# Attention and two expert layers in one kernel: ranking steps of the second layer later, its second phase in pieces, and another order of the last attention slots

## The chip, the cores and the metric

The kernel runs on one core of one Trainium2 chip. The metric is the time of one execution on the device, in microseconds (us). All matrix products run on TensorE (PE); VectorE (DVE), ScalarE (ACT) and GpSimd (POOL) do the elementwise work; SyncE (SP) issues most of the DMA transfers, POOL the indirect ones.

## The reference, cut to what matters

Three stages, each on the output of the one before. Attention has 2 batches, 8 heads, 576 positions and 64 features a head, with a causal mask and a decay bias; its output is read as 1152 tokens of 512 features.

```python
# stage 1: attention, per batch and head
scores = where(causal, -1e9, q @ k.T / 8 + minimum(bias(s), 0))
x = softmax(scores) @ v                    # -> x [1152, 512]

# stage 2: one expert a token, at most 288 tokens an expert, in token order
expert_idx = argmax(x @ w_gate, 1);  gate_w = softmax(x @ w_gate)[expert_idx]
y = relu(disp @ w1[e]) @ w2[e]             # E=8, D=512, F=1024
x = gate_w * y, rows scattered back        # 0 for a token that found no place

# stage 3: tokens and experts matched in order of falling logits
order = argsort(-(x @ w_gate2).flatten())
for idx in order:                          # token is free and the expert has under 144
    assign(token, expert)
out[mask] = relu(x[mask] @ w1[e]) @ w2[e]
```

## The kernel before, in words

Every engine runs its own instructions in the order in which the program issues them, and that order is written out by hand. There are three stages.

**Attention** goes in slots, one head each, numbered m = -7 to 18. The lists `ORDER[0]` and `ORDER[1]` (even and odd slots) name the pieces of a slot in their order: E0 to E3 are scores and their exponentials (`pE`, L528 on PE, `pf`, L536 on ACT), M and D the running maxima for a later head (`pM`, D on DVE at L488, which writes `rm`), G0 the scaling of `rm` on ACT (L494), V0 to V2 the product with v (`pog`, L559 to L564), R0 to R2 the normalization (`rs` L570, `rs` L573, `xs` L578 on DVE; R2 frees the `pog` bank for the V0 of the slot after). P0 and P1 make the second half of a split of the exponentials (`ph` L403, `pl` L414; `pl` is on POOL for some). X1 splits a finished head pair into two f16 halves, `XR`, one on ACT (L401), one on POOL (L414).

The gate of batch 0 is a generator, `gate0`, and one of its steps is run behind each piece of slots 11 and 12 (`step0`, GATE0 = 11); `WAITS` says behind which piece a marked step may go on. Its row work is on DVE: `gg` L703 to L709, the counts `cnt` L782, the ranking of experts to L789 (`eri`), then `slot` and the gate's inverse (L720 to L726). `cnt` reads the counts out of the `pog` bank. Then the tokens of batch 0 are scattered to `xd` in DRAM by five indirect DMAs (`scatter`, places in `SCATTER0`) in slots 13 to 15. `zero_fill` sets the DRAM buffers `xd` and `x2d` to zero, two transfers a slot (none in slot 9), on SP; `W0` says how many quarters of the first expert's weights are asked for after which slot, on the same queue, and `SPA` how many weight splits go behind a slot. A split makes `wh` (f16, ACT, L160) and `wl` (bf16, DVE, L164) of an f32 quarter `wf`, so that a product runs as three 16-bit passes (L1004 to L1006).

**First expert layer**: eight experts with 288 places, PE nearly without a break.

**Second expert layer**: eight experts with 144 places, taken in order of how soon they are full. The matching runs as phases p = 0 to 7 of the generator `work`. One phase multiplies indicators by gate rows (L1651 to L1667, into `px`; `g` is made by ACT L1659 and DVE L1661 out of `rowb`, L1224, which ACT copies from PE's transposes L1221), compares (L1869 to L1878), makes places (L1504 to L1512) and counts (L1885 on PE, `tot` L1888), finds which expert is full (`evi` L1679, read by SP to load weights), multiplies again for its tokens (L1518, L1902, `tok` L1715), which POOL gathers into `xg` (L1523), and PE transposes (`spread`, L1543, `xt` L1548).

An expert is 4 groups of 24 products into a hidden layer (L1004 to L1006), then the second layer, L1948, in 4 output blocks. In the first expert a block is 8 f32 products (16 records in the trace); with `halved` = 4 it is 12 f16 and 4 f32 products (20 records). Between these pieces `tick(k)` runs what a script says for place k (0 to 11 in the first product, 12 to 21 in the second): `w` is one step of `work`, `h` and `l` the next ACT and DVE part of a weight split, `s` and `t` the halves of the next expert's `spread`, `0` and `1` the halves of the last expert's output. `FIRST` is the script of the first expert, `THEN` that of all others.

## Time and profile before

| | us |
|---|---|
| three runs: lowest, median, highest | 442.37, 442.89, 448.96 |
| profiled execution, its own time | 441.93 |
| its span on the core | 440.1 |
| PE busy (share of the span) | 396.0 (90%) |
| DVE, ACT, POOL busy | 333.6, 261.8, 191.1 |
| mean granted TensorE clock | 0.973 |

The profile's times start at the span's start. Slot 11 begins at about 96.6 us, slot 12 at 102.1, 13 at 110.7, 14 at 118.0, 15 at 124.2; the first expert layer runs from 147.5 to about 290 us, and the second from 297.7 to 432 us. A matmul's record is longer than its distance to the next, because matmuls overlap: the distance of two starts is the time that one takes.

### The profile page before, as it was taken

To read this page: it belongs to the slowest core of one execution; us is meant where nothing else is said; L and a number is where in the kernel's file an instruction comes from. 1 tells how busy PE (TensorE), PEld (TensorE's weight loads), DVE (VectorE), ACT (ScalarE), POOL (GpSimd) and SP (SyncE) were. 2 spreads that over 40 slices of the span, in tenths; PEclk is the share of its full clock that TensorE was granted. 3 is DMA by queue.
4 is the path that set the end of the run, shared out by engine and by line. 5 is a ranking of instruction groups with operands and counts; after the bars stand their busy time and mean duration, and the time that the engine had idled before them with its cause. 6 is when DMAs were issued, how large, how long until landed. Compare 5 with 4: busy or idle time off the path is not lost.

```text
span 440.1 us, 13965 instructions
## 1 busy us (share of the span) xinstructions
PE 396.0 (90%) x5376; PEld 366.0 (83%) x5376; DVE 333.6 (76%) x955; ACT 261.8 (59%) x472; POOL 191.1 (43%) x306
## 2 busy tenths in 40 slices
PE   1679999998878799999999999869989999999994
PEld 1457888886766799999999999738879999999993
DVE  7889999989677377867778894858596878876730
ACT  4448888876482255556565853535476776766641
POOL 4397788875770702142044181522054244244121
PEclk9979999999899999999999999988989999999998
DMA  6797899952987869999999691188999697899511
GB/s 153 168 216 166 181 212 225 224 148 81 311 290 234 298 158 306 384 343 343 335 346 391 99 174 20 29 251 218 356 359 343 200 354 281 242 334 345 171 41 35
DMA packets 94399, 103.04 MB, mean 234 GB/s; under 512 B 56136, under 2 KB 63304, under 8 KB 94323
## 3 DMA queue, kind: packets, MB, share of 16 engines
q1 hardware_dynamic: 88931, 91.85, 71.6%
q0 software_dynamic: 4192, 9.91, 7.3%
q8 instruction: 44, 0.72, 0.7%
q10 hardware_dynamic: 1200, 0.30, 0.3%
q14 instruction: 32, 0.26, 0.2%
HBM read 81.42 MB, written 14.59 MB: 218 GB/s over the span
## 4 chain that ended last, share of the span: by engine, by line
PE 57%; DMA 14%; DVE 13%; issue 6%; ACT 4%; SPq 3%; POOL 2%; POOLq 0%; DVEq 0%; ACTq 0%
PE C L1061 11%; DMA xg<-x2d,tok 7%; PE A L1004 4%; PE A L1005 4%; PE A L1006 4%; PE pog L559 3%; PE C L1948 3%; PE pT L452 3%; DVE wl L164 3%; PE pM L476 2%; PE pE L528 2%; DMA wf<-in_moe_w_dram 2%; PE pE L529 2%; DVE wf L164 2%; PE A L1948 2%
## 5 line engine op out<-in xcount | busy, mean ns | idle before, releaser
L164 DVE TENSOR_TENSOR wl<-wf,wh 128x1024 bf16<-128x1024 f32 x64 | 77.0, 1222 | 22.7 <-ACT wh L160 22.2
L160 ACT ACTIVATE wh<-wf 128x1024 f16<-128x1024 f32 x64 | 65.7, 1050 | 18.5 <-DMA wf<-in_moe_w_dram 10.5
L1005 PE MATMUL A<-xt,wh 128*128 128x144 f16 (+4 forms) x288 | 59.5, 231 | 0.0
L1006 PE MATMUL A<-xt,wl 128*128 128x144 f16 (+4 forms) x288 | 59.5, 231 | 0.0
L1004 PE MATMUL A<-xt,wh 128*128 128x144 f16 (+4 forms) x288 | 59.5, 231 | 0.0
L1061 PE MATMUL C<-h,wf 128*128 128x160 f32 (+7 forms) x544 | 58.3, 269 | 0.0
L1176 POOL DMA_INDIRECT x2d<-xo,tix x14 | 22.9, 1638 | 71.2 <-DVE l L1193 26.5
L1004 PEld LDWEIGHTS <-wh 128*128 128x128 f16 x512 | 50.6, 99 | 2.2 <-PE pM L653 1.6
L1005 PEld LDWEIGHTS <-wh 128*128 128x128 f16 x512 | 50.4, 99 | 1.5 <-issue 1.0
L1006 PEld LDWEIGHTS <-wl 128*128 128x128 bf16 x512 | 50.5, 99 | 0.0
L536 ACT ACTIVATE pf<-pE,XB 128x512 f32<-128x512 f32 (+4 forms) x80 | 36.9, 514 | 10.5 <-PE pE L531 10.3
L414 POOL TENSOR_TENSOR pl<-pf,ph 128x512 f16<-128x512 f32 x30 | 35.6, 1196 | 11.4 <-DVE ph L403 8.8
L1972 POOL DMA_INDIRECT out_dram<-x2f,tok x14 | 16.2, 1160 | 55.4 <-ACT h L1012 26.3
L164 DVE TENSOR_TENSOR wf<-wf,wf 128x1024 bf16<-128x1024 f32 x30 | 35.7, 1218 | 2.6 <-ACT wf L160 2.6
L1523 POOL DMA_INDIRECT xg<-x2d,tok x16 | 24.9, 1556 | 26.3 <-PE A L1221 11.2
L1061 PEld LDWEIGHTS C<-h,wf 128*128 128x128 f32 x256 | 36.2, 190 | 0.0
L488 DVE CUSTOM_DVE_ANT_0 junk<-pM,cb 128x128 f16<-128x128 f32 (+4 forms) x80 | 32.1, 430 | 4.6 <-PE pM L478 3.9
L476 PE MATMUL pM<-al,ar 128*128 128x128 f16 (+2 forms) x96 | 26.5, 317 | 7.1 <-DVE rm L488 6.9
L1948 PE MATMUL C<-h,wf 128*128 128x144 f32 (+1 forms) x312 | 32.6, 260 | 0.0
L160 ACT ACTIVATE wf<-wf 128x1024 f16<-128x1024 f32 x30 | 31.3, 1051 | 0.0
L559 PE MATMUL pog<-vf,pf 128*128 128x65 f32 x180 | 29.1, 284 | 0.0
L1006 PE MATMUL C<-xt,wl 128*128 128x144 f16 x128 | 25.1, 229 | 0.0
(431 smaller groups left out, 1190.0 us busy)
## 6 DMA issues: line engine op xcount, KB each, us to landing
wf<-in_moe_w_dram SPq DMA_DIRECT2D x128, 512.0 KB
xd<-zero SPq DMA_DIRECT2D x18, 257.0 KB
cb<-cumd SPq DMA_DIRECT2D x16, 288.0 KB
x2d<-zero SPq DMA_DIRECT2D x9, 260.5 KB
kf<-in_k_dram SPq DMA_DIRECT2D x16, 128.0 KB
vf<-in_v_dram SPq DMA_DIRECT2D x16, 128.0 KB
qf<-in_q_dram SPq DMA_DIRECT2D x14, 128.0 KB
bl<-al SPq DMA_DIRECT2D x16, 72.0 KB
```

Of the source, the lines that this page charges most:

```text
L160: nc.scalar.activation(hi, src, AF.Copy)
L164: nc.vector.tensor_sub(lo, src, hi)
L414: (nc.gpsimd if ENG[name][i % 2] == "P" else nc.vector).tensor_sub(o, x, y)
L476: nc.tensor.matmul(o, AR[m][:, t * P:(t + 1) * P], AL[m][:, j0:j1], start=True, stop=not diag)
L488: nc.vector.tensor_tensor_reduce(junk[:w, :j1 - j0], o, CB[m][:w, j0:j1], 1.0, r if t == 4 and j0 == 0 else -3e38, OP.add, OP.max, r)
L536: nc.scalar.activation(d, o, AF.Exp, bias=x, scale=2.0 ** -13)
L559: nc.tensor.matmul(o, pf[:, c:c + P], VF[n % 4][:, j, h], start=False, stop=j == t)
L1004: nc.tensor.matmul(ph[:, g], wh[:, c, fs], xt[:, c], start=c == 0, stop=False)
L1005: nc.tensor.matmul(ph[:, g], wh[:, c, fs], xt[:, 4 + c], start=False, stop=False)
L1006: nc.tensor.matmul(ph[:, g], wl[:, c, fs], xt[:, c], start=False, stop=c == 3)
L1061: nc.tensor.matmul(py[:, g], a[:, f, d], b[:, f], start=k == 0, stop=k == len(terms) - 1)
L1948: nc.tensor.matmul(py[:, g], a[:, f, d], b[:, f], start=k == 0, stop=k == len(terms) - 1)
```

## The change

**Attention.** G0 stands behind D3 in both lists, so `rm` is scaled after the copies `al` and `ar`. The gate of batch 0 makes `slot` and the inverse only when slot 12 has reached its last piece, S, behind the normalization of that slot; the weights are asked for inside the gate, as soon as `eri` is known, four quarters, then 2 and 2 (`W0`); `x2d` is zeroed in slots 9 to 11 with 3 transfers each, not between the weights. The splits behind slots 13 to 15 are 2, 1, 1 (`SPA`), not 1, 1, 2. The next-to-last X1 goes before the fourth of the five scatters, not behind the fifth place.

**Second expert layer.** The w2 of the first expert comes in quarters of rows (2 x 512 values a partition), not of columns (8 x 128). Expert 1 is no longer `halved`: two splits fewer and f32 products in its second layer. Phase 1 is in pieces: its comparisons and counts stand between the halves of expert 0's spread, its places and tokens later. In expert 2 and after, a phase's products stand behind all four groups of the hidden layer (place 10), not behind three (place 8), and counts, tokens and the transposes L1221 are each 2 to 4 places later. A new script `SECOND` is for expert 1.

The diff, cut to its core:

```diff
-        if i // 2 == E:
+        if i == 2 * E:
             sl = (slice(None), slice(None), slice(c * f // 4, (c + 1) * f // 4))
...
-    second_splits = [(2 * E + i, part) for i in range(2 * E) for part in range(HALF2 // 2 if i % 2 else 4) if i != 1]
+    second_splits = [(2 * E + i, part) for i in range(2 * E) for part in range(HALF2 // 2 if i % 2 else 4) if i not in (1, 3)]
...
-    SPA = {13: 1, 14: 1, 15: 2}
+    SPA = {13: 2, 14: 1, 15: 1}
...
         yield from first_experts()
+        some_w(W0[GATE0 + 1])
         yield "loads"
         yield from gate_rows(0)
...
-    WAITS = {"products": (GATE0, "M2"), "sums": (GATE0, "R0"), "loads": (GATE0 + 1, "V2")}
+    WAITS = {"products": (GATE0, "M2"), "sums": (GATE0, "R0"), "loads": (GATE0 + 1, "S")}
-    W0 = {GATE0 + 1: 3, GATE0 + 2: 3, GATE0 + 3: 2}
+    W0 = {GATE0 + 1: 4, GATE0 + 2: 2, GATE0 + 3: 2}
...
-        if m in (GATE0, GATE0 + 1):
+        if GATE0 <= m < GATE0 + 3:
...
-        "E0 Q E1 K X1 M0 D0 V0 M1 V1 D1 X QE M2 VS XE E3 P0 D2 P1 QS E2 V2 R0 R1 G0 M3 T R2 D3 XG VT TE L LG G1 LV S".split(),
-        "E0 VS M0 V0 Q D0 M1 E1 D1 P0 P1 V1 X1 E3 K E2 QE M2 V2 D2 R0 M3 X T R1 G0 LG XE TE R2 D3 QS L S G1 VT XG LV".split(),
+        "E0 Q E1 K X1 M0 D0 V0 M1 V1 D1 X QE M2 VS XE E3 P0 D2 P1 QS E2 V2 R0 R1 M3 T R2 D3 XG VT TE G0 L LG G1 LV S".split(),
+        "E0 VS M0 V0 Q D0 M1 E1 D1 P0 P1 V1 X1 E3 K E2 QE M2 V2 D2 R0 M3 X T R1 LG XE TE R2 D3 G0 QS L S G1 VT XG LV".split(),
...
+                    if (m, name) == (NH - 2, "S"):
+                        x1(NPAIR - 2)
                     scatter(0, slice(n, n + 1))
...
-            x1(NPAIR - 2)
             first_ones()
...
-        if m >= 0 and m != 9:
-            zero_fill(2)
+        if m >= 0:
+            zero_fill(2 if m < 9 else 3)
...
+            if p == 1:
+                yield
+                in_turn(counts, ranked)
+                known(p)
+                yield
+                in_turn(places)
+                kept_ranks()
+            else:
+                in_turn(counts, [None] + left)
+                known(p)
...
-            halved = HALF2 if e else 0
+            halved = HALF2 if e > 1 else 0
...
-    FIRST = "w . lw . . w . w w w w . w . wh l w h st lh wl hll"
-    THEN = "w h l h l0 w w . w . h w1l h wl h . w l s tl h l"
+    FIRST = "w . l . . w w . . . . www w . wh l h w st wlh wl hll"
+    SECOND = ". . . . 0 w w w . . w 1 h wl h . wl h ls tl wh l"
+    THEN = "w h l h l0 w w . . . wh 1l h wl h . w l s tl wh l"
...
-    XT1[0] = spread(xg.pop(0), between=(3, 2))
+    XT1[0] = spread(xg.pop(0), between=(ranked_first, counted_first))
```

On DVE, in slot 12 at the gate of batch 0, one piece of the difference (`L578` is R2 of the head before, `L488` is D3):

```order
 L570 TENSOR_SCALAR rs<-pog 128x5
-L703 TENSOR_TENSOR gt_2168<-pog,OH 128x40
+L703 TENSOR_TENSOR gt_2172<-pog,OH 128x40
 L573 RECIPROCAL rs<-rs 128x5
-L705 TENSOR_REDUCE gg<-gt_2168 128x5
+L705 TENSOR_REDUCE gg<-gt_2172 128x5
+L578 TENSOR_TENSOR xs_168<-pog,rs 128x5x64
 L707 TENSOR_SCALAR gg<-gg 128x5
-L578 TENSOR_TENSOR xs_168<-pog,rs 128x5x64
-L709 SCALAR_TENSOR_TENSOR gg<-gg 128x5
 L488 ISA junk,rm_159<-pM,cb,rm_159 64x512
 L488 ISA rm_159 64x1
```

`xs` stands ahead of L707 now, and L709 behind the maxima, right before `cnt` L782.

On DVE at the start of expert 0 of the second layer, where phase 1 goes from its comparisons to its counts; before:

```order
L1507 TENSOR_SCALAR hq_5795<-r_5790 128x5
L1508 SCALAR_TENSOR_TENSOR hq_5795<-hq_5795,r_5790 128x5
L1509 TENSOR_TENSOR hq_5795<-hq_5795,Lr 128x5
L1510 TENSOR_TENSOR O_5796<-iota0f,hq_5795 128x360
L1512 TENSOR_TENSOR hq_5795<-Lr,hq_5795 128x5
L1504 TENSOR_TENSOR R_5797<-BA_5787,hq_5795 128x40 x2
L164 TENSOR_TENSOR wl_84<-wf_78,wh_83 128x4x256
L1888 TENSOR_TENSOR tot<-tot,px 128x8
L1676 TENSOR_SCALAR full<-tot 128x8
```

The same place now (`tot` is L1895 there, and `xt` L1548 belongs to expert 0's spread):

```order
L1869 TENSOR_REDUCE mx_5754<-px 128x5
L1871 SCALAR_TENSOR_TENSOR BA_5756<-mx_5754,Bo_5674 128x40
L1548 COPY xt<-A_5715 128x576
L1895 TENSOR_TENSOR tot<-tot,px 128x8
L1875 TENSOR_TENSOR own_5758<-px,BA_5756 128x40
L1676 TENSOR_SCALAR full<-tot 128x8
L1876 TENSOR_REDUCE nw_5760<-BA_5756 128x5
L1677 TENSOR_TENSOR nf<-full 128x8
L1877 TENSOR_REDUCE r_5759<-own_5758 128x5
L1678 ISA ej,evf<-nf,iota_73 128x8
```

The counts go on directly behind the comparisons; the places (L1507 to L1512, L1504) and a split stood between them, and come later.

On ACT around the start of expert 3 of the second layer, a steady one; before:

```order
L1224 ACTIVATE rowb<-A_6826 128x384
L1224 ACTIVATE rowb<-A_6830 128x256
L1548 COPY xt<-A_6856 128x576
L160 ACTIVATE wh_85<-wf_3046 128x4x256
L1954 ACTIVATE y<-C_6835 128x2x144
L160 ACTIVATE wf_3047<-wf_3039 128x1024
L1012 ACTIVATE h<-C_6896 128x2x144
L160 ACTIVATE wf_3047<-wf_3039 128x1024
L1967 ACTIVATE x2f<-D_6957,gq 72x512
L1012 ACTIVATE h<-A_6929 128x2x144
L1659 ACTIVATE g<-rowb,m_6725 128x640 x2
```

The same place now:

```order
L1548 COPY xt<-A_6808 128x576
L1224 ACTIVATE rowb<-A_6844 128x384
L1224 ACTIVATE rowb<-A_6848 128x256
L160 ACTIVATE wh_85<-wf_3046 128x4x256
L1972 ACTIVATE y<-C_6787 128x2x144
L160 ACTIVATE wf_3047<-wf_3039 128x1024
L1012 ACTIVATE h<-C_6857 128x2x144
L160 ACTIVATE wf_3047<-wf_3039 128x1024
L1985 ACTIVATE x2f<-D_6918,gq 72x512
L1012 ACTIVATE h<-A_6890 128x2x144
L1659 ACTIVATE g<-rowb,m_6716 128x640 x2
```

`rowb` went behind `xt`, to the border of two experts; `g` keeps its place among the rest, two groups of the hidden layer ahead of the products that read it, where it was one.

## Rows read from the trace of the kernel before

**Rows 1.** The page, busy time: us (share of the span) x instructions.
```profile
PE 396.0 (90%) x5376; PEld 366.0 (83%) x5376; DVE 333.6 (76%) x955; ACT 261.8 (59%) x472; POOL 191.1 (43%) x306
```

**Rows 2.** Busy time by stretches of 20 us: stretch, engines (instructions), PEclk, DMA share, GB/s.
```profile
100.00:120.00 20.00, 16.55 (x219) 13.68 (x216) 16.50 (x58) 9.75 (x23) 12.42 (x16) 0.91 0.58 176
120.00:140.00 20.00, 15.61 (x229) 13.01 (x228) 14.67 (x33) 12.63 (x23) 9.36 (x9) 1.00 0.77 256
...
320.00:340.00 20.00, 18.11 (x249) 17.69 (x247) 16.07 (x45) 13.34 (x21) 9.59 (x8) 0.91 1.00 352
```

**Rows 3.** PE's waits, 96 to 148 us: total, times, longest.
```profile
PE pog L562 <- DVE cnt L782: 1.7, 1, 1.7
PE pog L562 <- DVE xs L578: 1.4, 1, 1.4
...
PE pT L452 <- ACT XR L401: 1.3, 1, 1.3
```

**Rows 4.** Timeline of DVE, then POOL, slot 12: start, us, what.
```profile
103.65 1.04 DVE L709 SCALAR_TENSOR_TENSOR gg<-gg 128x5 f32<-128x5 f32 x1
...
111.20 0.92 DVE L724 TENSOR_SCALAR gg<-gg 128x5 f32<-128x5 f32 x1
...
103.28 1.40 POOL L414 TENSOR_TENSOR XR<-xs,XR 128x640 f16<-128x640 f32 x1
```

**Rows 5.** Timeline of SP's DMA queue, slots 12 and 13.
```profile
111.57 2.66 SPq L128 DMA_DIRECT2D wf<-in_moe_w_dram  x3
```

**Rows 6.** Timeline of ACT, slots 13 and 14.
```profile
120.37 1.06 ACT L160 ACTIVATE wh<-wf 128x1024 f16<-128x1024 f32 x1 [2.17 <-DMA wf<-in_moe_w_dram]
121.33 0.87 ACT L536 ACTIVATE pf<-pE,XB 128x512 f32<-128x512 f32 x2
```

**Rows 7.** Timeline of DVE, behind slot 15.
```profile
132.30 2.35 DVE L164 TENSOR_TENSOR wl<-wf,wh 128x1024 bf16<-128x1024 f32 x2
```

**Rows 8.** PE's waits, 295 to 345 us.
```profile
PE A L1543 <- DMA xg<-x2d,tok: 2.9, 2, 2.6
PE px L1667 <- DVE g L1661: 1.6, 1, 1.6
PE px L1518 <- DVE tot L1888: 0.9, 1, 0.9
PE A L1221 <- ACT xt L1548: 0.4, 1, 0.4
PE px L1667 <- ACT g L1659: 0.3, 1, 0.3
```

**Rows 9.** Timeline of DVE, then ACT, expert 0 of the second layer.
```profile
304.15 0.15 DVE L1679 TENSOR_SCALAR evi<-evf 128x1 int32<-128x1 f32 x1
...
315.25 1.06 ACT L160 ACTIVATE wh<-wf 128x1024 f16<-128x1024 f32 x1 [6.17 <-DMA wf<-in_moe_w_dram]
```

**Rows 10.** Busy time by stretches of 2 us, experts 0 and 1.
```profile
298.00:300.00 2.00, 2.00 (x43) 2.00 (x41) 2.00 (x4) 1.99 (x3) 0.00 (x0) 0.50 1.16 296
...
328.00:330.00 2.00, 2.00 (x20) 1.85 (x19) 1.90 (x14) 0.98 (x2) 0.45 (x2) 0.50 1.04 328
330.00:332.00 2.00, 2.00 (x19) 2.00 (x18) 1.94 (x9) 1.73 (x3) 0.36 (x1) 0.70 1.00 376
```

**Rows 11.** Timeline of PE: a phase's products in expert 0, in expert 3, and second-layer blocks.
```profile
308.29 0.18 PE L1845 MATMUL px<-tm,part 128*128 128x40 f16 x1
...
309.05 2.21 PE L1948 MATMUL D<-h,wf 128*128 128x144 f32 x16
...
360.58 0.18 PE L1845 MATMUL px<-tm,part 128*128 128x40 f16 x1
...
361.90 0.22 PE L1004 MATMUL C<-xt,wh 128*128 128x144 f16 x1
...
363.97 1.94 PE L1948 MATMUL C<-h,wf 128*128 128x144 f16 x20
```

**Rows 12.** Timeline of ACT, expert 3: the scaled gate rows.
```profile
360.16 1.54 ACT L1659 ACTIVATE g<-rowb,m 128x640 f16<-128x640 f32 x2
```

More of the change, by code (lines that the diff above doesn't have):

```diff
@@ L880, in tile_attention_moe_moe @@
                 step0(m, name)
-                if (m, name) == WAITS["loads"]:
-                    some_w(W0[m])
                 if (m, name) in SCATTER0:
                     n = SCATTER0.index((m, name))
+                    if n == 0:
+                        assert not held_up
+                        done(between)
+                    if (m, name) == (NH - 2, "S"):
+                        x1(NPAIR - 2)
                     scatter(0, slice(n, n + 1))
@@ L888, in tile_attention_moe_moe @@
         if m == NH - 2:
-            x1(NPAIR - 2)
             first_ones()
-        if m == GATE0 + 1:
-            assert not held_up
-            done(between)
-        elif m in W0:
+        if m in W0 and m > GATE0 + 1:
             some_w(W0[m])
@@ L1529, in tile_attention_moe_moe, with spread @@
     gates = []
-    def spread(xg, x=None, k=None, between=(0, 0)):
+    def spread(xg, x=None, k=None, between=(None, None)):
         if not k:
@@ L1545, in spread @@
             if between[h]:
-                warm(between[h])
+                between[h]()
         for k in ks:
@@ L1874, in phases, with kept_ranks @@
             nw = rw.tile([P, CT], F32, name="nw1")
-            nc.vector.tensor_tensor(own, pc, BA, OP.mult)
-            if not last:
-                nc.vector.reduce_sum(nw, BA, axis=AX.X)
-            nc.vector.reduce_sum(r, own, axis=AX.X)
+            ranked = [lambda: nc.vector.tensor_tensor(own, pc, BA, OP.mult),
+                      lambda: last or nc.vector.reduce_sum(nw, BA, axis=AX.X),
+                      lambda: nc.vector.reduce_sum(r, own, axis=AX.X)]
             O, R, places = slot_ones(r, BA, Lr[:, :, E], CT, 1)
-            in_turn(places)
-            nc.gpsimd.tensor_add(SL2, SL2, own)
-            nc.gpsimd.tensor_add(A, A, BA)
-            yield
+            def kept_ranks():
+                nc.gpsimd.tensor_add(SL2, SL2, own)
+                nc.gpsimd.tensor_add(A, A, BA)
+            if p == 1:
+                yield
+            else:
+                in_turn(ranked)
+                in_turn(places)
+                kept_ranks()
+                yield
             for t in range(CT):
@@ L1895, in phases @@
                         lambda: nc.vector.tensor_tensor(Lo, Lo, c3(pen), OP.add)] + ops
-            in_turn(counts, [None] + left)
-            known(p)
+            if p == 1:
+                yield
+                in_turn(counts, ranked)
+                known(p)
+                yield
+                in_turn(places)
+                kept_ranks()
+            else:
+                in_turn(counts, [None] + left)
+                known(p)
             if not last:
@@ L1905, in phases @@
             yield
+            if p == 1:
+                in_turn(left)
+                yield
     chk = rp.tile([P, 2, NTT, E], F32, name="chk")
@@ L2039, in gather_next @@
                 passed(999)
-    FIRST = "w . lw . . w . w w w w . w . wh l w h st lh wl hll"
-    THEN = "w h l h l0 w w . w . h w1l h wl h . w l s tl h l"
-    FIRST, THEN = (x.split() for x in (FIRST, THEN))
+    FIRST = "w . l . . w w . . . . www w . wh l h w st wlh wl hll"
+    SECOND = ". . . . 0 w w w . . w 1 h wl h . wl h ls tl wh l"
+    THEN = "w h l h l0 w w . . . wh 1l h wl h . w l s tl wh l"
+    SCRIPTS = [x.split() for x in [FIRST, SECOND] + [THEN] * (E - 2)]
     next(work)
@@ L2049, in tile_attention_moe_moe, with ranked_first, counted_first @@
     pop_hi()
+    for _ in range(3):
+        next(work)
+    pop_lo()
+    pop_hi()
     warm(WARM2[2])
-    XT1[0] = spread(xg.pop(0), between=(3, 2))
-    next(work)
-    next(work)
-    next(work)
-    pop_hi()
-    pop_lo()
-    moe2(lambda e, k: (THEN if e else FIRST)[k].strip("."), True)
+    def ranked_first():
+        next(work)
+        warm(2)
+    def counted_first():
+        next(work)
+        warm(2)
+    XT1[0] = spread(xg.pop(0), between=(ranked_first, counted_first))
+    next(work)
+    moe2(lambda e, k: SCRIPTS[e][k].strip("."), True)
     assert next(work, None) is None
@@ L2077, in again @@
                 xg[e + 1] = gather(tok[:, e + 1])
-            return THEN[k].strip(".")
+            return SCRIPTS[-1][k].strip(".")
         moe2(again)
```

## The prediction

> **What bounds the kernel now.** First the page: PE is busy for 396.0 of 440.1 us, more than any other engine [rows 1], so a step pays only where PE stands still or runs slowly. Next the table by stretches: PE is idle for 20 - 16.55 = 3.45 and 4.39 us of two stretches in the last attention slots, and for 1.89 us of one at experts 0 and 1 of the second layer, where the granted clock is also 0.91, as it is in the first of the three [rows 2]. The list of PE's waits then names who is late: in attention DVE (`cnt`, `xs`) and an `XR` copy on ACT [rows 3], in the second layer the gather, the scaled gate rows `g` and the counts `tot` [rows 8]. The change works on these places. I sum against the profiled execution, 441.93 us, 0.96 below the median of 442.89.
>
> **A, the last attention slots.** Three terms lie on PE's path.
>
> Slots 12 and 13. PE's V0 waits 1.7 us for `cnt` and, one slot on, 1.4 us for `xs` [rows 3]. Both readers of `pog` stand behind small gate steps on DVE. L709 takes 1.04 us, from 103.65 to 104.69, and `XR` on POOL ends at 103.28 + 1.40 = 104.68; L724 takes 0.92 us [rows 4]. These are operations on five numbers a partition, so I read the time as a wait for POOL. In slot 12 L709 goes behind the maxima (L488), past the end of `XR`, but `cnt` stays behind both: I give it 0.4. In slot 13 `slot`, L722, L724 and L726 leave the way of `xs`, about 1.1 us with the 0.92 as most of it. Together V0 of slot 13 comes 1.5 us sooner.
>
> This doesn't all survive: ACT's in-order queue has a weight split in slot 14, which stood 2.17 us for its DMA, with the next head's exponentials right behind it at 121.33 [rows 6]. Zeroing transfers stood between the weights' quarters, and the second three went out at 111.57 and after [rows 5]; now `x2d` is done in slots 9 to 11 and all four quarters are asked for at once. But two splits instead of one stand there now, and the second is 0.96 us of ACT. If the two quarters land by an estimated 117.4 to 118.2, the exponentials come 1.92 later, at 119.3 to 120.1 and so 1.2 to 2.0 sooner; if they land no sooner than before, they come 0.96 later. I take 1.2.
>
> Slots 14 to 16. PE waits 1.3 us for `XR` on ACT [rows 3], whose `xs` stands behind two `wl` splits of 2.35 us on DVE [rows 7]; one of them goes, 1.15. On POOL the other half of `XR` goes before one indirect scatter. I take 1.2 for both, and 2.4 for A; bounds 1.0 (the second term nothing) to 3.6 (all three whole, and PE's clock not falling behind its wait).
>
> The cost of the rest here is nothing: G0 moves behind two copies of the same ACT queue, covered by the two slots that lie between `rm` and the head that uses it, and `rm` is not among PE's longer waits [rows 3]; if that cover were gone, E0's exponentials behind G0 would wait for D3 in each slot. Nine zeroing transfers move to slots 9 to 11; the 16 DMA engines are 58% busy in the 20 us behind [rows 2].
>
> The Trainium skill (SBUF — State Buffer, section "Who interferes with whom") says that a DVE instruction with two SBUF inputs and a GpSimd instruction that reads SBUF lock each other out for the whole instruction, and that the order of issue decides. L709's end on `XR`'s end agrees. By that rule L707, now behind `xs`, meets the same `XR`; this is rival 3.
>
> **B, expert 0 of the second layer.** Phase 1's products, 309.05 - 308.29 = 0.76 us as phase 2's show [rows 11], now stand between the spread's halves, where PE has 2.6 us of wait for the gather [rows 8]: 0.8 off the path. The wait of 0.9 for `tot` goes, because the counts follow the comparisons directly (ten DVE steps of the places and a split stood between), and so `evi`, at 304.15 [rows 9], comes about 5 us sooner, and with it the weights of expert 1, for which ACT waited 6.17 us [rows 9]. That wait costs PE little in expert 0 itself: 0.4 for `xt` and 0.3 for the gather of phase 1 [rows 8]. It is off PE's path here and on it in C. Against this I set an estimate of 0.75: expert 0's first product now stands behind an `xt` that shares DVE with the comparisons. From 298 to 300 us PE ran at the lower of its two levels, 0.50 of 2.4 GHz, behind its wait for the gather, which cost 1.0 [rows 8, 10]; I take half of it to go, as PE has more to do before. Sum: 0.8 + 0.9 + 0.7 + 0.5 - 0.75 = 2.15; I take 2.1. Bounds: 0.5 (only products and `xt`, with the start 0.75 later) to 3.3 (all of it, the clock too). The tokens of phase 1 come later within the expert, and the gather goes with them: by the order of the places it lands an estimated 0.5 us before its transposes, so this is the thinnest cover in the change.
>
> The rows of w2 in runs of 2 KB, where it was 512 B, only matter if the loads are late at the start; the transfer of 298 to 300 us ran at 296 GB/s with the engines full, against 376 at 330 to 332 [rows 10]. 2 MB at the one and the other differ by 1.5 us, which no PE wait shows: I put it at nothing; it is part of the cover above.
>
> **C, expert 1.** PE waits 1.6 us for DVE's `g` and 0.3 for ACT's [rows 8], and then its clock falls: 0.50 and 0.70 in the next 4 us, which loses 1.0 + 0.6 [rows 10]. Together 3.5. DVE and ACT are late there because the splits came late (6.17 us) and pile up. With earlier weights, two splits fewer on each and the products one group later, I expect all of it to go. The price is the second layer in f32: a block takes 2.21 us as 16 f32 records and 1.94 as 20 of both kinds [rows 11], 4 x 0.27 = 1.1. The net is 2.4; with the products' own group shorter by the 0.56 of D it is 2.9. I take 2.6; bounds 1.5 (1 us of wait stays) to 3.1.
>
> **D, experts 2 to 4.** In expert 3 a phase's products take 361.90 - 360.58 = 1.32 us where 0.76 is enough [rows 11], because ACT's `g` ends at 361.70 [rows 12]. The wait list doesn't show it, since it lies inside the group. Products after four groups, not three, come one group later; `g` also comes later, since `rowb` moves to the experts' border. On ACT three splits of 0.96 [rows 6] and `rowb`, `y`, two `h` and `x2f`, an estimated 2.1 together, then stand ahead of `g`, which puts its start 5.0 us and its end 5.0 + 1.54 = 6.5 us behind the expert's start; PE's products begin about as late, behind 96 products and the last output's transposes (6.45 by the distances of their starts), and read the late half last. So 0.56 goes three times, 1.7. I take 1.4, between nothing (ACT a further 0.6 late) and 2.0.
>
> Elsewhere (slots before 11, the first expert layer, the last three experts) I see no wait that is touched: 0, with 0.3 either way.
>
> Sum: 2.4 + 2.1 + 2.6 + 1.4 = 8.5, so 441.93 - 8.5 = 433.4 profiled, and 442.89 - 8.5 = **434.4** against the median.
>
> **Rivals.** (1) All steps give their full count: 3.1 + 2.7 + 2.9 + 1.7 = 10.4, 432.5. For it: each was followed through the order on its engines. Against it: each stretch has a next engine that is nearly late.
> (2) The start of the second layer gives back what it gets: the gather of phase 1 is late by 2 to 3 us, PE waits and its clock falls as after the 1.6 us wait [rows 8, 10]. B is then 0 or below and C 1: 442.89 - 2.4 - 1.0 - 1.4 = 438. For it: the cover is an estimated 0.5 us. Against: the weights are out of the gather's way sooner.
> (3) Attention gains nothing: `XR` takes the port ahead of L707, which then stands until 104.7 as L709 did [rows 4], and ACT's two splits wait for their quarters ahead of the exponentials, as one did [rows 6]: 442.89 - 6.1 = 436.8. For it: the splits sit in front. Against: the zeroing transfers are gone from their queue.
> (4) Slower: `g` in experts 2 to 4 comes late. From a lateness of some 1.6 us on, PE loses it and then the clock, as in expert 1, 3.5 us each time [rows 8, 10]. With A and B as forecast, C at 0 and D at +10.5 it is 442.89 - 4.5 + 10.5 = 449. It decides at 1.6 us of slip in ACT's chain; I count none, with a slack near zero.
> (5) The moved pieces only change who is waited for, and the time stays at 442.
>
> **How the numbers follow.** Forecast 0.52 (432.8 to 436.5), rival 1 0.18, rival 2 0.12, rival 3 0.11, rival 4 0.04, rival 5 0.03. The range from 431 to 439 leaves out rivals 4 and 5, the tails of rival 2 and what goes beyond the full count. Two per cent, about what a measurement of this kernel can tell from no change, is 434.0: rival 1 and two fifths of the forecast are below it, 0.40; slower by 2% (451.7) is the upper end of rival 4 alone, 0.02; the rest is 0.58.
>
> **What would show it.** A: no wait of PE for `xs` in slot 13, clock 1.00 from 112 to 118, exponentials of slot 14 about a microsecond earlier, less idle time at 120 to 140. B: phase 1's products before the first L1004, no wait for `tot`, `evi` near 299, no long ACT wait for `wf`. C: no L1667 wait in expert 1 and no half clock; 16 f32 records a block. D: 0.76 us from L1845 to the next product. It is wrong if a new wait for `xg` shows in expert 0's end, if ACT's `wh` of slot 14 starts later than 118, or if `px` waits for ACT in experts 2 to 4.

## The result and the profile after

The changed kernel takes 436.74 us (median of 4 runs, 435.51 to 437.73), the kernel before 442.76 us in the runs beside it: 6.0 us less, a ratio of 0.984 with an interval of 0.980 to 0.988. That is a gain of 1.6 per cent, clear of the noise. The forecast was 434.4, in a range of 431 to 439; the measured time lies in that range, 2.3 us above the forecast and just above the band of 432.8 to 436.5 that the prediction gave its main case. The profiled execution of the changed kernel is the slowest of its four, 437.73, so its rows account for 4.2 us; two places below, where it lost 3.6 us, may be why it gained less than the median.

The stretches that answer to [rows 2], in the same columns. The third held expert 1 before; now it holds most of expert 1 and the start of expert 2:

```profile
100.00:120.00 20.00, 17.00 (x246) 14.08 (x244) 16.32 (x57) 12.35 (x28) 15.12 (x17) 1.00 0.69 250
120.00:140.00 20.00, 16.50 (x228) 13.40 (x228) 15.06 (x48) 9.81 (x20) 8.00 (x8) 1.00 0.45 140
...
320.00:340.00 20.00, 19.81 (x284) 19.61 (x281) 13.82 (x43) 13.81 (x24) 6.96 (x7) 1.00 1.03 344
...
380.00:400.00 20.00, 18.46 (x270) 18.11 (x266) 14.48 (x38) 12.15 (x19) 8.22 (x11) 1.00 0.95 307
```

PE is fuller in the three stretches that the change aimed at, by 0.45, 0.89 and 1.70 us, and the clock is whole in all of them in this trace. The last row is a new hole of 1.5 us, where before had PE busy for the whole 20.

To see where the time went, PE's timeline of both traces is cut at instructions that both have: the first scores of a head (`pE`, 512 columns), the first L1004 of a layer or expert, L1221, and the first L1543 of a spread. Lengths in us, worked out from those starts; each column is one execution:

| from, to | before | after | difference |
|---|---|---|---|
| start to slot 11 | 96.61 | 96.00 | -0.61 |
| slot 11 | 5.45 | 5.40 | -0.05 |
| slot 12 | 8.67 | 7.86 | -0.81 |
| slot 13 | 7.25 | 4.83 | -2.42 |
| slot 14 to first expert layer | 29.55 | 30.00 | +0.45 |
| first expert layer, to its last L1221 but one | 125.97 | 128.27 | +2.30 |
| from there to the spread of expert 0 | 22.21 | 22.33 | +0.12 |
| spread to expert 0 | 1.94 | 2.85 | +0.91 |
| expert 0 | 21.36 | 18.01 | -3.35 |
| expert 1 | 19.94 | 17.18 | -2.76 |
| experts 2, 3, 4 | 16.70, 16.70, 16.16 | 16.66, 16.67, 16.12 | -0.11 |
| expert 5 | 15.00 | 15.12 | +0.12 |
| expert 6 | 14.97 | 16.87 | +1.90 |
| expert 7 | 15.51 | 15.50 | -0.01 |

The sum is -4.32. The start to slot 11 is nothing that the change made: in the runs below it lies between 95.6 and 96.8, whatever was edited.

In attention, PE's waits that answer to [rows 3] (line waited for: total, times, longest):

```profile
PE pT L452 <- POOL XR L414: 1.2, 1, 1.2
PE pog L562 <- DVE cnt L782: 1.0, 1, 1.0
PE pog L562 <- DVE xs L578: 0.8, 2, 0.6
...
PE pT L452 <- ACT XR L401: 0.5, 1, 0.5
```

`cnt` costs 0.7 less, `xs` in slot 13 0.3 where it was 1.4 (the rest of its 0.8 is another slot's), ACT's `XR` 0.8 less; POOL's `XR` costs 0.5 more. The rows that answer to [rows 4], DVE's and then POOL's timeline:

```profile
102.30 0.37 DVE L707 TENSOR_SCALAR gg<-gg 128x5 f32<-128x5 f32 x1
...
103.25 0.77 DVE L709 SCALAR_TENSOR_TENSOR gg<-gg 128x5 f32<-128x5 f32 x1
...
111.59 0.43 DVE L724 TENSOR_SCALAR gg<-gg 128x5 f32<-128x5 f32 x1
...
100.25 2.39 POOL L414 TENSOR_TENSOR pl<-pf,ph 128x512 f16<-128x512 f32 x2 [1.41 <-DVE ph L403]
102.61 1.40 POOL L414 TENSOR_TENSOR XR<-xs,XR 128x640 f16<-128x640 f32 x1
```

L709 ends at 104.02, where `XR` ends (104.01): it is still held, for less time because it starts later. In all 14 traces of this case it ends within 0.03 us of `XR`. L707 ends at 102.67, with the end of `pl` (102.64), and is not held by `XR`. The maxima L488 stood behind L709, and so behind `XR`; now they run while `XR` does. Before, then now:

```profile
104.62 0.73 DVE L488 CUSTOM_DVE_ANT_0 junk<-pM,cb,rm 64x512 f16<-64x512 f32 x1
...
102.58 0.73 DVE L488 CUSTOM_DVE_ANT_0 junk<-pM,cb,rm 64x512 f16<-64x512 f32 x1
```

The weights, on SP's queue and then on ACT, where [rows 5] and [rows 6] stood:

```profile
107.53 5.13 SPq L128 DMA_DIRECT2D wf<-in_moe_w_dram  x8
...
116.47 2.00 ACT L160 ACTIVATE wh<-wf 128x1024 f16<-128x1024 f32 x2 [2.15 <-DMA wf<-in_moe_w_dram]
118.38 1.40 ACT L536 ACTIVATE pf<-pE,XB 128x512 f32<-128x512 f32 x3
```

All eight quarters go out in one stretch from 107.53. ACT still waits 2.15 us, but ends that wait 3.9 us sooner by the time of the trace; 1.5 of this is that slot 13 starts sooner, and counted from there it is 9.64 - 7.21 = 2.4. With two splits in front the exponentials come at 118.38, not 121.33.

In the second layer PE waits 2.8 us between 294 and 345 us, against 6.1 us in [rows 8]; the list starts at 294 here, because the gather's wait now ends at 294.69:

```profile
PE A L1543 <- DMA xg<-x2d,tok: 2.4, 1, 2.4
PE px L1667 <- DVE g L1661: 0.4, 1, 0.4
```

So the long wait for the first gather is still there. It stands ahead of the spread, and phase 1's products stand behind it, not in it. PE at the start of expert 0, before and then now:

```profile
295.71 0.43 PE L1543 MATMUL A<-ident,xg 72*128 72x72 f16 x8 [2.58 <-DMA xg<-x2d,tok]
...
294.69 0.43 PE L1543 MATMUL A<-ident,xg 72*128 72x72 f16 x8 [2.38 <-DMA xg<-x2d,tok]
294.96 0.19 PE L1845 MATMUL px<-tm,part 128*128 128x40 f16 x1
...
295.72 0.59 PE L1721 MATMUL C<-iotat,ident 128*128 128x512 f16 x2
296.15 0.61 PE L1543 MATMUL A<-ident,xg 72*128 72x72 f16 x8
296.57 0.31 PE L1892 MATMUL px<-BA,ones 128*128 128x8 f16 x5
```

The products take 295.72 - 294.96 = 0.76 us of the start and the counts (L1892) 0.16; this is the 0.91 by which the start grew. The clock is at its lower level behind the gather's wait as it was before:

```profile
296.00:298.00 2.00, 2.00 (x21) 1.33 (x20) 1.46 (x12) 0.64 (x1) 0.42 (x2) 0.55 1.04 386
298.00:300.00 2.00, 2.00 (x22) 2.00 (x21) 1.97 (x9) 0.00 (x0) 0.08 (x1) 0.59 1.00 342
```

That loses 2 x 0.45 + 2 x 0.41 = 1.7 us; before it was 0.77, 0.50 and 0.88 from 296 to 302, 1.7 as well.

`evi`, at 304.15 in [rows 9], is now at 297.97, and no wait of ACT for `wf` in experts 0 and 1 is longer than 1.96 us where one was 6.17. The granted clock, 0.50 at 328 to 330 in [rows 10], is whole:

```profile
328.00:330.00 2.00, 2.00 (x23) 1.98 (x23) 1.90 (x6) 1.33 (x3) 1.04 (x2) 1.00 1.06 392
```

Last, a phase's products in expert 3, for [rows 11], on PE and with them DVE's last part of `g`:

```profile
355.83 0.18 PE L1845 MATMUL px<-tm,part 128*128 128x40 f16 x1
...
356.84 0.28 PE L1667 MATMUL px<-Bo,g 128*128 128x8 f16 x5 [0.36 <-DVE g L1661]
...
357.10 0.61 PE L1982 MATMUL D<-identf,y 128*72 128x128 f32 x4
...
353.60 2.36 DVE L164 TENSOR_TENSOR wf<-wf,wf 128x1024 bf16<-128x1024 f32 x2
355.86 0.46 DVE L1013 SCALAR_TENSOR_TENSOR h<-A,h 128x288 f16<-128x288 f32 x1
356.23 0.55 DVE L1661 TENSOR_SCALAR g<-rowb,m 128x640 f16<-128x640 f32 x1
...
354.36 1.56 ACT L1659 ACTIVATE g<-rowb,m 128x640 f16<-128x640 f32 x2
```

From 355.83 to 357.10 it is 1.27 us, against 1.32 before. ACT's `g`, which I had taken for the last, was done at 355.92; PE waits for DVE's. Before, DVE's was the earlier of the two, done at 361.35 where ACT's was done at 361.70 [rows 12]:

```profile
360.80 0.55 DVE L1661 TENSOR_SCALAR g<-rowb,m 128x640 f16<-128x640 f32 x1
```

### The profile page after: what moved, and what is told of

Read it like the earlier page. It is cut to its first block, busy times and chain, and to the rows that moved or that the text cites. A ratio compares the mean times of both kernels' runs of the same rounds, so it can differ in the third digit from the quotient of the medians.

```text
span 435.9 us, 13913 instructions
## 1 busy us (share of the span) xinstructions
PE 394.1 (90%) x5359; PEld 365.3 (84%) x5359; DVE 327.3 (75%) x951; ACT 259.1 (59%) x470; POOL 189.2 (43%) x306
## 4 chain that ended last, share of the span: by engine, by line
PE 57%; DVE 15%; DMA 14%; issue 5%; ACT 3%; POOL 2%; SPq 1%; another core or an unknown queue 1%; POOLq 0%; ACTq 0%; DVEq 0%
PE C L1061 11%; DMA xg<-x2d,tok 8%; PE A L1004 4%; PE A L1006 4%; PE A L1005 4%; PE C L1966 4%; DVE wl L164 4%; PE pog L559 3%; PE pT L452 3%; DMA kf<-in_k_dram 2%; PE pM L476 2%; DVE wf L164 2%; PE A L1966 2%; PE D L1966 2%; DMA wf<-in_moe_w_dram 2%
## 5 line engine op out<-in xcount | busy, mean ns | idle before, releaser
L164 DVE TENSOR_TENSOR wl<-wf,wh 128x1024 bf16<-128x1024 f32 x64 | 78.0, 1233 | 28.6 <-ACT wh L160 27.7
L1005 PE MATMUL A<-xt,wh 128*128 128x144 f16 (+4 forms) x288 | 61.0, 235 | 0.0
L1006 PE MATMUL A<-xt,wl 128*128 128x144 f16 (+4 forms) x288 | 60.9, 235 | 0.0
L1004 PE MATMUL A<-xt,wh 128*128 128x144 f16 (+4 forms) x288 | 60.9, 235 | 0.0
L1004 PEld LDWEIGHTS <-wh 128*128 128x128 f16 x512 | 51.0, 100 | 3.3 <-remote 1.7
L1990 POOL DMA_INDIRECT out_dram<-x2f,tok x14 | 19.5, 1392 | 54.0 <-ACT h L1012 19.0
L488 DVE CUSTOM_DVE_ANT_0 junk<-pM,cb 128x128 f16<-128x128 f32 (+4 forms) x80 | 32.1, 429 | 4.5 <-PE pM L478 3.8
L164 DVE TENSOR_TENSOR wf<-wf,wf 128x1024 bf16<-128x1024 f32 x28 | 33.4, 1219 | 2.6 <-ACT wf L160 2.6
L1966 PE MATMUL C<-h,wf 128*128 128x144 f16 (+1 forms) x304 | 32.7, 261 | 0.0
L1523 POOL DMA_INDIRECT xg<-x2d,tok x16 | 19.7, 1234 | 24.2 <-DMA x2d<-x2f,tix 6.2
L160 ACT ACTIVATE wf<-wf 128x1024 f16<-128x1024 f32 x28 | 29.3, 1055 | 0.0
L1004 PE MATMUL C<-xt,wh 128*128 128x144 f16 x128 | 24.6, 226 | 0.0
```

The source lines that it names most:

```text
L160: nc.scalar.activation(hi, src, AF.Copy)
L164: nc.vector.tensor_sub(lo, src, hi)
L488: nc.vector.tensor_tensor_reduce(junk[:w, :j1 - j0], o, CB[m][:w, j0:j1], 1.0, r if t == 4 and j0 == 0 else -3e38, OP.add, OP.max, r)
L1004: nc.tensor.matmul(ph[:, g], wh[:, c, fs], xt[:, c], start=c == 0, stop=False)
L1005: nc.tensor.matmul(ph[:, g], wh[:, c, fs], xt[:, 4 + c], start=False, stop=False)
L1006: nc.tensor.matmul(ph[:, g], wl[:, c, fs], xt[:, c], start=False, stop=c == 3)
```

## The experiments

All were timed beside the kernel before on the same chip; times of different groups are not compared directly, because the chips differ by 4 us (before: 444.16 in the first group, 440.14 in the second, 443.67 in the third). Intervals are of the ratio to the kernel before. The unedited changed kernel ran in the second group alone. The kernel before was traced once, outside these groups, so a length in a trace that is set against it can differ by chip and by execution as well as by the edit.

**First group: the two halves of the change, and the script.**

`attn_only` has the attention part and none of the rest (the edits of the diff from `SPA` to the zeroing).

> The kernel before with the attention part of the change alone. Theory (the gain of each part stands by itself): first expert layer starts 2.8 us sooner than before beside the common offset of slot 11, second layer unchanged, about 440 us or less if no clock drop follows at the wtl wait (L1250/L1262). Rival (the attention gain is given back in the first layer, because the transposed weights wtl are late by the same amount): PE waits for wtl about 0.5 us, clock falls to about 0.7 around 260, and the time is that of before, 442 to 443.

Measured 441.34 us, 0.993 (0.990 to 0.996). From slot 11 to the first expert layer it takes 48.26 us against 50.92 before: -2.66. The first expert layer takes 127.82 against 125.97: +1.85. Experts 1 and 2 of the second layer are as before (19.94, 16.70), with the waits of [rows 8] back; expert 0 takes 22.08 and its start 3.15, 0.7 and 1.2 us more than before, though no edit touches them: the clock is at half from 282.5 to 300 us. So in this trace the part gains what the trace of the changed kernel says and gives two thirds of it back in the first layer. The timed runs don't show that loss: 444.16 - 441.34 is 2.8 us, about the whole gain. What takes it in the trace is the clock, by stretches of 2 us:

```profile
262.00:264.00 2.00, 2.00 (x23) 2.00 (x21) 0.12 (x2) 0.40 (x1) 0.00 (x0) 0.53 0.32 18
264.00:266.00 2.00, 2.00 (x24) 2.00 (x23) 1.03 (x4) 0.00 (x1) 0.00 (x0) 0.61 0.00 0
```

PE runs near its lower level, 1.2 of 2.4 GHz, for some 3.5 us, which loses 2 x 0.47 + 2 x 0.39 = 1.7 us. Ahead of it PE did products of 8 and 16 columns with transposed weights (L1260, L1262), and waited 0.3 us for the transposing DMA (`wtl`). The changed kernel has the same rows, 0.52 and 0.63; before has 1.00 there.

`moe2_only` has the part of the second layer and none of attention.

> The kernel before with the part of the second expert layer alone. Theory: expert 0 about 18.0 us and expert 1 about 17.2 us long, start 0.9 us later against its gather, experts 2 to 4 unchanged: 5.2 us less, about 437.6. Rival (the two parts need each other): expert 0 or 1 longer by over 1 us than in the changed kernel.

Measured 439.12 us, 0.990 (0.986 to 0.994). Expert 0 takes 17.61 and expert 1 17.18, the start behind the gather 3.26, experts 2 to 4 16.67, 16.67, 16.12; attention 50.92, as before, and no clock drop at 262 to 266. The rival falls: the two parts don't need each other. The ratios of the two halves, 0.993 and 0.990, multiply to 0.983, next to the 0.984 of the whole.

Its attention part is that of before, and this shows something on slot 13. Before, PE's wait for `xs` was followed by the lower clock; here PE waits as long, and the clock stays whole. The clock of the two stretches before, then PE's wait (1.4 us before, [rows 3]) and the same stretches in `moe2_only`:

```profile
112.00:114.00 2.00, 1.24 (x17) 1.23 (x17) 1.97 (x9) 0.16 (x1) 0.19 (x2) 0.69 1.03 293
114.00:116.00 2.00, 2.00 (x19) 1.55 (x17) 0.33 (x2) 1.00 (x3) 1.86 (x5) 0.50 0.83 269
...
112.59 0.19 PE L562 MATMUL pog<-vh,ph 128*128 128x65 f16 x1 [1.39 <-DVE xs L578]
112.00:114.00 2.00, 1.41 (x27) 1.22 (x27) 2.00 (x8) 0.10 (x1) 0.26 (x1) 1.00 0.82 254
114.00:116.00 2.00, 2.00 (x31) 1.92 (x31) 0.90 (x3) 1.94 (x5) 1.86 (x5) 1.00 0.80 283
```

Slot 13 takes 5.68 us here and 7.25 before, and yet slot 11 to the first layer takes 50.92 in both: what the whole clock saved was waited off behind slot 13.

`then_old` has the old script in experts 2 to 7:

```diff
-    THEN = "w h l h l0 w w . . . wh 1l h wl h . w l s tl wh l"
+    THEN = "w h l h l0 w w . w . h w1l h wl h . w l s tl h l"
```

> The changed kernel with the script of before for experts 2 and on (products behind three groups, L1221 at place 16). Theory (DVE's last part of g sits behind two weight splits and is as late as the products, so moving the products gained nothing): experts 2 to 4 keep 16.7 us each, time within 0.5 us of the changed kernel. Rival (the moved products gain what was forecast and something else hides it): 1.4 to 1.7 us slower than the changed kernel.

Measured 439.67 us, 0.991 (0.988 to 0.994). Experts 3 and 4 take 16.70 and 16.17, as the theory had it, but expert 2 takes 19.76, 3.1 more. PE's waits in expert 2:

```profile
PE px L1667 <- DVE g L1661: 1.3, 1, 1.3
PE px L1667 <- ACT g L1659: 0.4, 1, 0.4
```

and then the clock falls to 0.71 and 0.50. In expert 1 the script `SECOND` still makes the rows L1221 at the expert's border, while expert 2's products stand early: the old wait of expert 1 is back, one expert on. So both theories were short. The moved products gain nothing in a steady expert, but they go with the rows at the border; in expert 2, rows made at the border with the products left early cost 3 us.

`g_early` puts the ranking step that makes DVE's third part of `g` (and ACT's first) ahead of the weight splits:

```diff
-    THEN = "w h l h l0 w w . . . wh 1l h wl h . w l s tl wh l"
+    THEN = "w h wl h l0 . w . . . wh 1l h wl h . w l s tl wh l"
```

> The changed kernel with one step of ranking earlier in experts 2 and on: DVE's third part of g (and ACT's first) go ahead of the second-layer weight splits, the products stay behind four groups. Theory (DVE's last part of g decides): no wait inside the products, 0.8 us from the first to the last of them, and experts 2 to 4 about 0.4 to 0.5 us shorter each, 1.2 to 1.5 us in all. Rival (ACT's g or the products' own length decides): 1.27 us as in the changed kernel, no gain.

Measured 439.33 us, 0.990 (0.987 to 0.993). Experts 2 and 3 take 16.14 and 16.15, 0.52 less each, but experts 4, 5 and 6 take 16.49, 17.10 and 16.42: behind them PE waits 1.9 us for an `xt` on DVE and 1.2 for a step of the kernel's last check of the matching. The 1.9 us, at 384.74, is the stand of PE, ACT and DVE together that the last section shows, and other scripts have it too, so it can't be put down to this edit. The mechanism stands, its gain is not seen in the time; the same edit is taken to three experts alone in the next group.

**Second group.**

`after_again` is the changed kernel unedited.

> The changed kernel once more, beside the runs that follow. Theory (a clock drop at 262 to 265 us, behind the products with wtl, belongs to the new timing of the attention part): granted clock under 0.7 there again, first products of expert 0 to L1221 about 128 us against 126 before. Rival (it was an accident of one execution): no drop, 126.

Measured 434.25 us, 0.987 (0.982 to 0.992). The first layer takes 124.85 us and the clock is whole from 260 to 266. So the drop doesn't belong to the attention part alone. In this group's four traces PE also lacks two waits at the first products of the first layer that all other traces have: one for `cnt` (L923), 1.4 us in nine of them and 0.7 in `w2_cols`, and about 1 us for which the profile shows no releaser. The layer starts and ends with another timing.

`wtl_warm` adds three products of 384 columns ahead of the second half of the products with `wtl`:

```diff
+        for _ in range(3 if part else 0):
+            nc.tensor.matmul(wide[e][:, 16 * E:], ident, iotat[:, :512 - 16 * E], start=True, stop=True)
```

> The changed kernel with 3 more products of 384 columns, into an unused part of the same bank, ahead of the second half of the products with wtl (two experts have them, about 0.5 us each, one of them partly inside the wait for wtl). Theory (PE's thin work there lets the clock fall, and that takes back most of what the attention part won): clock 1.00 from 262 to 266, 1.0 to 1.5 us less than the changed kernel. Rival (the drop comes whatever PE does there): drop stays, 0.5 to 1 us more than the changed kernel.

Measured 433.83 us, 0.985 (0.982 to 0.989), first layer 125.04. It tells nothing about the drop, since the unedited kernel's trace on this chip has none; the first layer is 0.2 us longer with the added products.

`g_early3` has the script of `g_early` in experts 2 to 4 alone:

```diff
-    SCRIPTS = [x.split() for x in [FIRST, SECOND] + [THEN] * (E - 2)]
+    EARLY = "w h wl h l0 . w . . . wh 1l h wl h . w l s tl wh l"
+    SCRIPTS = [x.split() for x in [FIRST, SECOND] + [EARLY] * 3 + [THEN] * (E - 5)]
```

> The changed kernel with the earlier step for g in experts 2 to 4 only. Theory (DVE's last part of g decides inside the products): experts 2, 3 and 4 take 16.15, 16.15 and 15.6 us, 1.5 us less in all, and experts 5 to 7 are as in the changed kernel. Rival (what is gained is lost at the next expert's start, because the splits come later): the wait for xt stays at 1 us or more somewhere behind, no gain in the sum.

Measured 432.58 us, 0.983 (0.979 to 0.987), beside 434.25 and 0.987 for the unedited one. Experts 2 to 4 take 16.14, 16.15 and 15.60, 1.56 less in all, expert 5 the same 15.12, expert 6 16.30 against 16.37. PE's products and DVE's `g` in expert 2:

```profile
336.37 0.18 PE L1845 MATMUL px<-tm,part 128*128 128x40 f16 x1
...
337.13 0.61 PE L1982 MATMUL D<-identf,y 128*72 128x128 f32 x4
...
334.14 0.55 DVE L1661 TENSOR_SCALAR g<-rowb,m 128x640 f16<-128x640 f32 x1
334.60 2.35 DVE L164 TENSOR_TENSOR wf<-wf,wf 128x1024 bf16<-128x1024 f32 x2
```

0.76 us and no wait, with `g` ahead of the splits. ACT's last part of `g` ends as far behind the first of these products as in the changed kernel, 0.09 us (336.46 - 336.37; 355.92 - 355.83), so it is DVE's part that made the difference:

```profile
335.62 0.84 ACT L1659 ACTIVATE g<-rowb,m 128x640 f16<-128x640 f32 x1
```

The theory holds in the trace. The median is the lowest of this group, 1.7 us under the unedited kernel's and 0.7 under the next; the intervals overlap, so the traces show the step and the timing only agrees.

`e1_halved` splits expert 1 again:

```diff
-            halved = HALF2 if e > 1 else 0
+            halved = HALF2 if e else 0
-    SECOND = ". . . . 0 w w w . . w 1 h wl h . wl h ls tl wh l"
+    SECOND = ". h l h l0 w w w . . w 1 h wl h . wl h ls tl wh l"
```

(and `second_splits` leaves out 1 alone, as before).

> The changed kernel with expert 1 split again (two more splits on ACT and DVE, f16 passes for half of its second layer). Theory (the old wait in expert 1 came from weights that landed late, so the unsplit second layer only costs now): expert 1 takes 16.1 us instead of 17.2, no wait for g, 1 us less in all. Rival (the two splits themselves make g late): a wait of 1 us or more for g in expert 1 or 2, a clock drop behind it, and 2 to 3 us more.

Measured 433.24 us, 0.986 (0.981 to 0.991). Expert 1 takes 17.19 against 17.18. Neither theory: its second layer gets back the 1.1 us, and the two splits put DVE's parts of `g` behind, so the products take 318.83 - 317.15 = 1.68 us where they took 0.76. The unsplit second layer is an even trade.

**Third group.**

`late5` and `early_late` have the script of before in experts 5 to 7, the second with `g_early3`'s script in 2 to 4:

```diff
+    LATE = "w h l h l0 w w . w . h w1l h wl h . w l s tl h l"
+    SCRIPTS = [x.split() for x in [FIRST, SECOND] + [THEN] * 3 + [LATE] * (E - 5)]
```

> The changed kernel with the script of before for experts 5 to 7 alone. Theory (phase 7 needs no g, so its later products only delay the last expert's weights): experts 5 and 6 take 15.0 us each and ACT's wh in expert 6 doesn't wait for its DMA; experts 2 to 4 stay at 16.66. About 1 us less than the changed kernel. Rival: ACT still waits 1 us or more for wf in expert 6.

> The changed kernel with the earlier step for g in experts 2 to 4 and the script of before for experts 5 to 7. Theory (DVE's last part of g costs 0.5 us each in experts 2 to 4, and the later counts of phase 7 make the last expert's weights late): experts 2 to 4 take 16.15, 16.15 and 15.6 us, experts 5 and 6 15.0 each, no wait of PE in experts 5 and 6; 2 to 3 us less than the changed kernel. Rival (expert 6 loses by accident of each execution): expert 6 still over 15.5.

Measured 436.86 us, 0.986 (0.982 to 0.989), and 436.61 us, 0.984 (0.981 to 0.988). Experts 2 to 4 are as foretold (16.69, 16.65, 16.12 and 16.15, 16.15, 15.60), but expert 6 takes 16.85 and 16.40, not 15.0. What the theory named did go: ACT no longer waits for `wf` in expert 6, where the changed kernel waits 1.58 us and its second trace 2.26:

```profile
400.72 1.06 ACT L160 ACTIVATE wh<-wf 128x1024 f16<-128x1024 f32 x1 [2.26 <-DMA wf<-in_moe_w_dram]
```

(that is `after_again`; PE waits 0.9 for the `h` behind it). Others came in its place, 1.4 us for `Q` of that last check in `early_late` and a stand of 2.0 us in `late5`. My theory on expert 6 falls as an account of its length. The two kernels differ by the script of experts 2 to 4 alone; the traces have it 1.56 us shorter there, the medians only 0.25 apart. So the time that this step saves is not confirmed by a timing.

`zero_old` zeroes two transfers a slot again, so that zeroing transfers stand between the requests for the first weights (four quarters, two zeroing transfers, two quarters, two, two):

```diff
-        if m >= 0:
-            zero_fill(2 if m < 9 else 3)
+        if m >= 0 and m != 9:
+            zero_fill(2)
```

> The changed kernel with two zeroing transfers a slot again (none in slot 9), so that x2d is still being zeroed while the first weights land. Theory (the zeroing transfers held the first weights back): ACT's splits of slot 14 start 1 us or more later against slot 13's first scores than in the changed kernel (7.2 us behind), and the exponentials with them. Rival (asking sooner is what counts, the zeroing is beside it): within 0.4 us of 7.2.

Measured 438.52 us, 0.989 (0.984 to 0.993). ACT's splits start at 117.95, 8.48 us behind slot 13's first scores, against 7.21 in the changed kernel and 7.23 to 7.89 in the other three of this group:

```profile
117.95 2.00 ACT L160 ACTIVATE wh<-wf 128x1024 f16<-128x1024 f32 x2 [3.43 <-DMA wf<-in_moe_w_dram]
119.86 1.40 ACT L536 ACTIVATE pf<-pE,XB 128x512 f32<-128x512 f32 x3
```

In this one trace the zeroing held the weights back by 0.6 to 1.3 us of the 2.4 that ACT's wait ends sooner, counted from slot 13. The rest was not tested by itself; the first request is no sooner, 1.73 us ahead of slot 13's first scores before and now (109.00, 107.53).

`w2_cols` has `i // 2 == E` again, so that the first w2 comes by columns.

> The changed kernel with the first w2 of the second layer in column quarters again (runs of 512 B). Theory (its loads lie under the gather's wait): expert 0 and its start within 0.3 us of the changed kernel's 2.9 and 18.0 us. Rival (the loads share the DMA engines with phase 1's gather and expert 1's weights): a wait for xg or wf of 0.5 us or more in experts 0 and 1.

Measured 437.67 us, 0.986 (0.981 to 0.991). Expert 0 takes 17.94, expert 1 17.18, the start 3.60 (3.29 to 3.59 in the others of the group); PE waits for nothing in experts 0 and 1, and ACT 1.3 us once for `wf`. The rows of w2 were worth nothing that PE shows in this trace.

## Why the prediction was right, and where not

**A, forecast 2.4, measured 2.83** (2.66 alone). The sum is near, the pieces came out otherwise than sized, so the nearness is in part luck. In slot 12 the forecast "past the end of `XR`" was wrong: L709 stays locked until `XR` ends, and the gain, 0.8, comes from `xs` going first and from the maxima L488, which now run while `XR` does. In slot 13 the wait for `xs` fell by 1.1, as sized; the rest of the 2.4 is the clock of 112 to 116, which fell in the trace of before and not in this one. `moe2_only` shows that this part was worth nothing to the whole. The traces point to the weights instead, though no run tests it alone: the exponentials of slot 14 start 121.33 - 96.61 = 24.7 us behind slot 11's first scores before, 24.6 in `moe2_only`, and 118.38 - 96.00 = 22.4 now. The weights came at 116.47, 0.9 ahead of my estimate, of which 0.6 is that slot 11 started sooner in this trace. How much of the 1.2 us behind slot 14 was kept the traces don't say: ACT's `XR` costs 0.8 less, POOL's 0.5 more, though its part of X1 now stands ahead of the fourth scatter and not behind it, and slot 14 to the first layer takes 30.00, between the 29.55 of before and the 31.13 of `moe2_only`.

One trace doesn't size A. In the eleven traces with the whole attention part slot 11 to the first layer takes 46.55 to 49.69 us, which is 1.2 to 4.4 less than before. In seven of the eleven the clock falls to 0.50 for some 7 us between 118 and 132; the changed kernel's first trace is one of the four without.

The rule of locked ports that the prediction quotes (the Trainium skill, SBUF — State Buffer, section "Who interferes with whom") is about a DVE instruction with two SBUF inputs and a GpSimd instruction that reads SBUF. L709 has two, and this trace agrees: it ended with `XR` again, 104.02 against 104.01. L707 has one, so the rule as quoted does not name it; the trace has it end with POOL's `pl` (102.67, 102.64), ahead of `XR`. Rival 3 didn't come, though the measured 436.74 is next to its 436.8: that the numbers meet says nothing for it, since attention did gain.

**B, forecast 2.1, measured 3.35 - 0.91 = 2.44.** Here too the sum is near and its steps are not. The waits for `tot`, `xt` and phase 1's gather are gone, 1.6 us as sized. But the 0.8 for the products was a misreading: PE's wait of 2.6 us for the gather stands ahead of the spread's first half, not between its halves, and 2.4 of it stays. The products stand behind that wait, so they are paid in the start, as most of its 0.91. The 0.75 set there was for an `xt` beside the comparisons, and PE shows no wait for it; that the two errors are of one size is luck. The 0.5 of clock didn't come, 1.7 us are lost there before and now. So some 0.8 of the 2.44 has no step to stand for it. The size also depends on the pair of traces: on one chip, start and expert 0 take 25.23 in `attn_only` and 20.87 in `moe2_only`, 4.4 less, with the clock at half for longer in the former. Rival 2 didn't come: PE waits for no second gather in the changed kernel.

**C, forecast 2.6, measured 2.76.** The wait for `g` and the half clock went. The reason that I gave in part, two splits fewer, is not it: `e1_halved` has the splits, no wait of 1 us and no half clock in expert 1, and the same 17.18. The rows and products moved together are a part of it; `then_old` brings the wait and the half clock back by parting the two. What the earlier weights did was not tested by itself.

**D, forecast 1.4, measured 0.11: the step that failed.** It said that ACT's `g` decides, and followed ACT's queue alone; ACT did end as computed, 6.5 us behind the expert's start (355.92 - 349.39). DVE's third part of `g` stands behind a split (`wl`) that waits for ACT's `wh`, and then behind 2.36 us of weight splits. With `rowb` moved it ends 7.4 us behind the expert's start where it was 5.7; the products begin at 6.4 where they began at 4.9. So it is delayed by about as much as the products were moved. `g_early3` shows the price, 1.56 us, by taking it out of that place.

**What the sum left out** is 1.7 of clock in the first layer and 2.0 in experts 5 and 6 of this execution. "0, with 0.3 either way" for the rest of the kernel was wrong in size: nothing there is touched, but its clock and its fine timing differ from one execution to the next. Without these two the profiled execution would be at 434.0, 0.6 from the 433.4 of the sum, or 434.6 without the start to slot 11, which was 0.6 shorter by no edit. The other runs of the changed kernel are up to 2.2 us faster, but with no trace of them it is not shown that these losses are absent there. Since the terms erred by +0.4, +0.3, +0.2 and -1.3, the total was nearer than its steps. Of the 2.5 us by which the medians gained less than forecast (6.0 against 8.5), D is 1.3; the other 1.2 is not accounted for.

## What to carry to other kernels

A product waits for the last of its operands: where one operand is made in parts on two engines, follow both queues to the end before you move it, because the engine that was last before need not be the last after. When a producer and its reader are moved, move both, and check the reader's other producers; here half of a move cost 3 us and the whole of it gained nothing until one more instruction was taken out of line. Before you count work as hidden in a wait, look on which side of the wait it stands. And a gain ahead of a long PE-bound stage is not banked until the stage's clock has been read, in more than one trace: the unedited kernel had the drop in one and not in the other.

## What the runs showed of the hardware

The clock of a stretch that no edit touches differs from one execution to the next. From 262 to 266 us it was 1.00 in before and in `moe2_only`, whole in all four kernels of the second group and in `late5`, and between 0.50 and 0.96 in the seven others, which all have the attention part. `late5` and the second group's four have it too, so that part alone doesn't decide. PE's work ahead of it, the thin products, is the same in all but `wtl_warm`; it ends between 258.0 and 264.6 us, and in the traces without the drop the clock is also whole in the 4 us behind it. What decides is not settled. Nor does a wait's length decide: 1.4 us for `xs` in slot 13 was followed by 0.69 and 0.50 before, and by 1.00 in `moe2_only`. Over whole runs of one kernel, the one before in the first group, the mean granted clock lies between 0.954 and 0.976 in 22 of 23.

In expert 6 of the changed kernel PE, ACT and DVE stood together for some 2 us, with nothing that the profile shows to release them:

```profile
399.06 0.22 PE L1005 MATMUL D<-xt,wh 128*128 128x144 f16 x1 [1.54 <-issue]
...
398.55 0.46 DVE L1548 COPY xt<-A 128x576 f16<-128x576 f16 x1 [2.13 <-PE A L1966]
...
399.35 0.41 ACT L1972 ACTIVATE y<-A 128x288 f32<-128x288 f32 x1 [2.33 <-remote]
```

DVE's and ACT's inputs were ready at 396.4 and 397.5, when the products that make them had ended. `late5` and `zero_old` have the same at the same instruction, and `g_early` has it one expert earlier; there the profile puts PE's wait down to DVE's `xt`, and DVE and ACT stand at least as long. Before, `attn_only`, `moe2_only`, `then_old` and `e1_halved` have no such stand, and expert 6 takes 14.9 to 15.0 us there, though `moe2_only` and `e1_halved` have the new script in experts 5 to 7. Returning the scripts of those experts did not remove it in `late5`. So the script doesn't decide it, and its cause stays open.
